# The last group's division in a mixer-attention kernel: sums moved by DMA, division on VectorE, eight jobs kept in halves of score buffers

## The chip, the core and the metric

The kernel runs on one core of one Trainium2 chip. The metric is device time in microseconds (us) of one execution; lower is better. Five engines of the core work side by side, each through its own queue in order: TensorE (PE, matmuls into PSUM), VectorE (DVE), ScalarE (ACT), GpSimd (POOL) and SyncE (SP, which here only issues DMAs). PSUM is used here as eight banks of 128 x 512 float32.

## The reference

Two kinds of blocks alternate, twice each with the same weights, on `x` of 2048 tokens by 512 channels; each block gets a layer norm of `x`, and its result is added to `x`.

```python
def _A_ref(x, wq, wk, wv, wo):              # 32 heads of 16, one shared key and value head
    q = (x @ wq).reshape(B, S, H, Dh).transpose(0, 2, 1, 3)
    k, v = x @ wk, x @ wv
    p = softmax(einsum("bhqd,bkd->bhqk", q, k) * Dh ** -0.5)
    o = einsum("bhqk,bkd->bhqd", p, v)
    return o.transpose(0, 2, 1, 3).reshape(B, S, H * Dh) @ wo
def _B_ref(x, w1, b1, w2, b2):              # token mixing: the MLP runs over the 2048 tokens
    h = layernorm(x)
    u = gelu(einsum("bsd,sf->bdf", h, w1) + b1)      # F = 1792
    return (einsum("bdf,fs->bds", u, w2) + b2).transpose(0, 2, 1)

x = A_x
x = x + _A_ref(layernorm(x), ...); x = x + _B_ref(layernorm(x), ...)
x = x + _A_ref(layernorm(x), ...); x = x + _B_ref(layernorm(x), ...)
```

## The kernel before

All tokens stay in SBUF as 16 row tiles `x0` to `x15` of 128 x 512. A float32 product is made of three matmuls: each operand is split into a rounded first part (a cast) and the rest (a subtract), and the product of the two rests is left out.

**Attention.** 32 groups (4 blocks of 512 queries by 8 groups of 4 heads) each make scores into double banks (`bank2`, tag `sc`, three buffers of two banks each, so six banks), exponentials on ACT, and sums into one of the two remaining banks (`bank`, tags `ac0` and `ac1`). The sums hold for each head the weighted values and the sums of weights in alternating rows. When a group's sums are done, `finish` copies them to SBUF (`ev`, line 696), and two DMAs move even and odd rows apart into a tile `o` for two groups: `o[:, 0]` has values, `o[:, 1]` the sums of weights (line 704). `division` then makes, for four slices of 128 columns, a reciprocal, a product, a cast and a subtract on DVE, and leaves them as `hl`. `project` multiplies `hl` by `wo` for one row tile and adds it to `x` on DVE (lines 762 and 765).

**The mixer's first product** begins during attention. Its unit is a half job: six matmuls that take one tile of `w1` (256 tokens by 128 columns, `w1r`, 128 KB by DMA) and two normed row tiles `hb`; two half jobs with the same 128 columns of `u` make a job, which is added by DVE into `uacc` (`ua`, line 1023). `following` is called after each half job: it splits the weight tile three half jobs ahead (in the tail a cast on ACT and a subtract on POOL, lines 1000 and 1002) and issues the load of the one seven ahead. There are 84 half jobs (42 jobs) for the first three blocks of tokens (`self.inner`); the 28 half jobs of the last block need its normed rows and come afterwards.

**The tail.** The methods run in the order in which they are written, and every engine takes its part of that order. `Mixer.rest`, called once per layer, does what is left after the last scores: the two remaining row tiles of the last projection but one (in a bank of `ac`), the last sums, the nine jobs that are left (66 to 82), the division of the last two groups, the last projection, the norm of the last four row tiles, and then the loop over the last block (`pu_l`, 168 matmuls), followed by the second product (`py`).

The last two groups go another way than the others there. `finish` keeps their `ev`, and `last_rows` moves even and odd rows apart by matmuls with columns of the identity into two score buffers (line 733), once for each group, the second time after four jobs. `last_division` copies the values on ACT, inverts on DVE from PSUM, multiplies and subtracts on POOL and casts on ACT (lines 744 to 750). The jobs run between these steps, each added to `ua` as soon as it is done, but for the last three. The last norm takes for each row tile a norm on DVE, a cast on ACT and a subtract on DVE or POOL in turn (lines 1121 to 1125).

Of the kernel before, what the change touches and what calls it, by code (L numbers as in the profile page):

```python
# [8 lines left out]
F32 = mybir.dt.float32  # L9
# [9 lines left out]
P = 128  # L19
S, D, H, DH, F = 2048, 512, 32, 16, 1792  # L20
NB = 4
# [31 lines left out]
def kernel(  # L53
# [612 lines left out]
    class Attention:  # L666
        def __init__(self, layer):
            self.l = layer
            self.pp = pool(f"weights{layer}", side="right")
            self.ohl, self.acc, self.pend = {}, {}, []  # L670
            self.drained, self.finished, self.late = 0, [], []
# [19 lines left out]
        def finish(self, i):  # L691
# [5 lines left out]
            if i >= NB * NG - 2:  # L697
                self.late.append(ev)
                return
# [26 lines left out]
        def last_rows(self):  # L726

            if not hasattr(self, "rows"):
                self.rows = [bank2(f"rows{self.l}_{k}")[:, 0, :] for k in range(2)]
                self.moved = 0  # L730
            r = 64 * self.moved
            for k in (1, 0):
                nc.tensor.matmul(  # L733
                    self.rows[k][r : r + 64, :], ident[:, k:P:2], self.late[self.moved],
                    start=True, stop=True, skip_group_check=True,
                )
            self.moved += 1

        def last_division(self):

            p, n, m = self.pool, self.l, NB * ND - 1
            o, d = (p.tile([P, 2, QB], F32, tag="o", bufs=2, name=f"o{n}_l{k}")[:, 0, :] for k in range(2))
            hl = self.ohl[m] = p.tile([P, 2, QB], F32R, tag="hl", bufs=2, name=f"hl{n}_{m}")
            nc.scalar.copy(o, self.rows[0])
            for t in range(4):
                c = slice(t * P, (t + 1) * P)
                nc.vector.reciprocal(d[:, c], self.rows[1][:, c])
                nc.gpsimd.tensor_tensor(o[:, c], o[:, c], d[:, c], op=ALU.mult)  # L748
                nc.scalar.copy(hl[:, 0, c], o[:, c])
                nc.gpsimd.tensor_tensor(hl[:, 1, c], o[:, c], f32(hl[:, 0, c]), op=ALU.subtract)  # L750
# [148 lines left out]
    class Mixer:  # L899
# [160 lines left out]
        def projection(self, att, which):  # L1060
# [3 lines left out]
            att.project(parts, t, bank(which, f"po{n}_{parts[0]}_{t}"))  # L1064
# [15 lines left out]
        def rest(self, att):  # L1080
# [4 lines left out]
            def job(pu=None):  # L1085

                j = self.done // 2
                if pu is None:
                    pu = bank(j, f"pu{n}_{self.done}")
                self.product(pu, stop=False)  # L1090
                self.following()
                r, f = self.product(pu, start=False)
                self.following()
                return pu, r - 1, f

            while self.projections:
# [321 lines left out]
```

## Time and profile before

| | |
|---|---|
| median of three runs | 2607.62 us (2606.88 to 2608.09) |
| the profiled execution's own time | 2608.36 us |
| its span, first to last instruction | 2606.2 us |
| mean granted TensorE clock | 0.994 |
| PE busy | 2567.8 us, 99% |
| ACT busy | 2122.6 us, 81% |
| DVE busy | 818.2 us, 31% |
| POOL busy | 142.5 us, 5% |

A row of a timeline has the start and the duration in us, the engine, the line of the kernel, the operation, what it writes and reads, and how many were merged; in brackets stands how long the engine was idle before it and what ended that. `PEld` is the loading of weights, which lies beside matmuls. A table by windows has for each window its length, then busy time and number of instructions of PE, PEld, DVE, ACT and POOL, the granted clock (1.00 is full), the busy share of the DMA engines and GB/s. In the rows of one line, three numbers with slashes are the shortest, median and longest duration in ns.

### The profile page before, as it was taken

What the parts mean: (1) busy time and instruction counts of PE and PEld (TensorE: products, weight loads), DVE (VectorE), ACT (ScalarE), POOL (GpSimd) and SP (SyncE); (2) the same over time, 40 slices, a digit from 0 to 9 for tenths busy, and PEclk for the clock granted to TensorE, in tenths of its full rate; (3) what the DMA queues carried; (4) which work ended last, traced back from release to release, by engine and by line L of the source; (5) the groups of instructions that cost most, each with busy time, mean ns of one, the idle gap of its engine ahead of it and who ended that gap; (6) DMA issues with size and microseconds to landing.
All of it is one profiled execution on the core that took longest, in us unless ns stands there. A gap on an engine that the chain in (4) does not pass through costs nothing. (4 is left out here: it accounts for less than half of the span.)

```text
span 2606.2 us, 41310 instructions
## 1 busy us (share of the span) xinstructions
PE 2567.8 (99%) x16168; PEld 1244.7 (48%) x16168; DVE 818.2 (31%) x1847; ACT 2122.6 (81%) x2368; POOL 142.5 (5%) x209
## 2 busy tenths in 40 slices
PE   7999999999999999999999999999999999999999
PEld 6344333444344444478873333434443444445887
DVE  6122242223222432254441222322242223323432
ACT  5889999999999999763239999999999999995511
POOL 2000000000000000141000000000000000002300
PEclk8999999999999999999999999999999999999999
DMA  3221201111111111034423110111111111101343
GB/s 98 67 64 48 62 27 42 30 42 32 38 30 38 31 40 30 19 99 117 130 60 106 53 47 28 31 38 30 38 30 38 30 38 33 42 25 37 114 124 96
DMA packets 167631, 138.24 MB, mean 53 GB/s; under 512 B 17378, under 2 KB 132096, under 8 KB 167168
## 3 DMA queue, kind: packets, MB, share of 16 engines
q1 hardware_dynamic: 167424, 135.48, 18.0%
q8 instruction: 131, 2.15, 0.4%
q14 instruction: 76, 0.62, 0.1%
HBM read 95.57 MB, written 24.12 MB: 46 GB/s over the span
## 5 line engine op out<-in xcount | busy, mean ns | idle before, releaser
L780 ACT ACTIVATE p<-sc 128x1024 f32<-128x1024 f32 x2048 | 1918.0, 1030 | 115.9 <-PE sc L773 115.9
L786 PE MATMUL acc<-p,vaug 128*32 128x512 f32 x8192 | 1012.6, 599 | 0.0
L773 PE MATMUL sc<-qs,kst 51*128 51x512 f32 x4096 | 724.2, 439 | 11.8 <-ACT p L780 3.4
L773 PEld LDWEIGHTS sc<-qs,kst 51*128 51x128 f32 x4096 | 325.8, 184 | 650.4 <-ACT p L780 378.0
L786 PEld LDWEIGHTS acc<-p,vaug 128*32 128x32 f32 x8192 | 227.3, 109 | 447.6 <-issue 407.3
L1195 PE MATMUL py<-u,w 128*128 128x512 f32 x1344 | 307.6, 390 | 0.0
L1195 PEld LDWEIGHTS py<-u,w 128*128 128x128 f32 x1344 | 251.9, 188 | 52.3
L1015 PE MATMUL pu<-hb,w 128*128 128x512 f32 x984 | 265.9, 409 | 0.4 <-POOL w L1002 0.4
L1015 PEld LDWEIGHTS pu<-hb,w 128*128 128x128 f32 x984 | 173.8, 188 | 85.0 <-issue 50.8
L1183 ACT CAST w<-w2r 128x896 fp32r<-128x896 f32 x64 | 60.3, 945 | 182.0 <-PE py L1195 170.3
L1023 DVE TENSOR_TENSOR ua<-ua,pu 128x512 f32<-128x512 f32 x54 | 37.0, 688 | 405.1 <-PE pu L1015 405.1
L1002 POOL TENSOR_TENSOR w<-w1r,w 128x256 fp32r<-128x256 f32 x86 | 68.4, 809 | 1699.6 <-ACT w L1000 1698.4
L765 DVE TENSOR_TENSOR x<-x,po 128x512 f32<-128x512 f32 x64 | 44.0, 688 | 306.9 <-PE po L762 306.9
L716 DVE RECIPROCAL o<-o 128x128 f32<-128x128 f32 x120 | 113.5, 946 | 12.3 <-DMA o<-ev 12.3
L696 DVE COPY ev<-acc 128x512 f32<-128x512 f32 x64 | 44.1, 689 | 214.1 <-PE acc L786 214.1
L1021 DVE COPY ua<-pu 128x512 f32<-128x512 f32 x28 | 19.4, 692 | 286.3 <-PE pu L1015 286.3
L1184 DVE TENSOR_TENSOR w<-w2r,w 128x896 fp32r<-128x896 f32 x64 | 71.5, 1119 | 104.7 <-ACT w L1183 104.6
L762 PE MATMUL po<-wo,hl 128*128 128x512 f32 x360 | 100.7, 413 | 1.6 <-DVE x L765 1.6
L353 PE MATMUL pq<-hT,wq 128*128 128x512 f32 x336 | 89.9, 417 | 0.0
L1015 PE MATMUL pu_l<-hb,w 128*128 128x512 f32 x336 | 82.0, 404 | 2.9 <-POOL hb L1125 1.7
L431 DVE CAST q<-pq 128x512 fp32r<-128x512 f32 x24 | 16.6, 692 | 208.8 <-PE pq L353 163.7
L762 PEld LDWEIGHTS po<-wo,hl 128*128 128x128 f32 x360 | 62.7, 188 | 36.3 <-issue 20.3
(166 smaller groups left out, 1048.7 us busy)
## 6 DMA issues: line engine op xcount, KB each, us to landing
w1r<-in_B_w_dram SPq DMA_DIRECT2D x224, 128.0 KB
w2r<-in_B_w_dram SPq DMA_DIRECT2D x64, 448.0 KB
qs<-qd SPq DMA_DIRECT2D x384, 64.0 KB
qd<-q SPq DMA_DIRECT2D x64, 256.0 KB
o<-ev SPq DMA_DIRECT2D x120, 128.0 KB
x<-in_A_x_dram SPq DMA_DIRECT2D x16, 256.0 KB
out_dram<-x SPq DMA_DIRECT2D x16, 256.0 KB
wqr<-in_A_wq_dram SPq DMA_DIRECT2D x4, 512.0 KB
```

What stands on the lines that cost most here:

```text
L353: yield nc.tensor.matmul(out, a, c, start=(k == 0), stop=(k == len(terms) - 1))
L696: nc.vector.tensor_copy(ev, acc)
L716: nc.vector.reciprocal(o[:, 1, c], o[:, 1, c])
L762: nc.tensor.matmul(po, a, c, start=(k == 0), stop=(k == 3 * len(parts) - 1))
L773: nc.tensor.matmul(sc[:, j, :], kst[kt // 4][rows, kt % 4 * P : (kt % 4 + 1) * P], qs[i % NQ][rows, j0 // 2, :], start=True, stop=True,)
L780: nc.scalar.activation(pt, sc, AF.Exp, scale=0.25)
L786: nc.tensor.matmul(self.acc[i][c : c + 32, :], vaug[:, kt].rearrange("p d k -> p (d k)"), pt[:, j, :], start=(kt == 0), stop=(kt == NKT - ...
L1002: eng.tensor_tensor(w[:, 1], raw, f32(w[:, 0]), op=ALU.subtract)
L1015: nc.tensor.matmul(pu, a, c, start=(start and k == 0), stop=(stop and k == 5))
L1183: nc.scalar.copy(w[:, 0], raw)
L1184: nc.vector.tensor_tensor(w[:, 1], raw, f32(w[:, 0]), op=ALU.subtract)
L1195: nc.tensor.matmul(py, a, d, start=(c == 0 and f == 0 and k == 0), stop=(c == 1 and f == NFH - 1 and k == 2),)
```

## The change

- `finish` treats the last two groups as all others: their sums go by two DMAs each into the shared tile `o`. `last_rows` is gone.
- `last_division` works on `o` in SBUF: reciprocal, product and subtract on DVE, the cast on ACT. It is a generator: one slice of columns is issued before a job and one after each of its half jobs, so its steps stand between those of two jobs.
- In `rest` the second of the remaining row tiles of the projection takes a score bank and not the bank of the first one.
- One job is added at once. The other eight are kept (`late`): two in `ac` banks (`pu_a`, `pu_b`) and six in halves of three score buffers (`pu_m`, `pu_l` twice). Two of the eight stand before the last projection and six behind it.
- The last projection runs as four row tiles in a row, two to a score buffer.
- The last norm goes by pairs of row tiles. Casts and subtracts are on DVE, but for one cast on ACT; after each pair four of the kept jobs are added.

```diff
@@ finish
-            if i >= NB * NG - 2:
-                self.late.append(ev)
-                return
             if i % 2 == 0:
                 self.o = p.tile([P, 2, QB], F32, tag="o", bufs=2, name=f"o{n}_{i}")
@@ last_rows is left out; last_division
-            o, d = (p.tile([P, 2, QB], F32, tag="o", bufs=2, name=f"o{n}_l{k}")[:, 0, :] for k in range(2))
+            o = self.o
             hl = self.ohl[m] = p.tile([P, 2, QB], F32R, tag="hl", bufs=2, name=f"hl{n}_{m}")
-            nc.scalar.copy(o, self.rows[0])
-            for t in range(4):
-                c = slice(t * P, (t + 1) * P)
-                nc.vector.reciprocal(d[:, c], self.rows[1][:, c])
-                nc.gpsimd.tensor_tensor(o[:, c], o[:, c], d[:, c], op=ALU.mult)
-                nc.scalar.copy(hl[:, 0, c], o[:, c])
-                nc.gpsimd.tensor_tensor(hl[:, 1, c], o[:, c], f32(hl[:, 0, c]), op=ALU.subtract)
+            cols = [slice(t * P, (t + 1) * P) for t in range(4)]
+
+            def second(c):
+                nc.vector.tensor_tensor(hl[:, 1, c], o[:, 0, c], f32(hl[:, 0, c]), op=ALU.subtract)
+
+            for t, c in enumerate(cols):
+                nc.vector.reciprocal(o[:, 1, c], o[:, 1, c])
+                nc.vector.tensor_tensor(o[:, 0, c], o[:, 0, c], o[:, 1, c], op=ALU.mult)
+                nc.scalar.copy(hl[:, 0, c], o[:, 0, c])
+                if t:
+                    second(cols[t - 1])
+                yield
+            second(cols[3])
+            yield
@@ projection
-            att.project(parts, t, bank(which, f"po{n}_{parts[0]}_{t}"))
+            name = f"po{n}_{parts[0]}_{t}"
+            att.project(parts, t, bank2(name)[:, 0, :] if which is None else bank(which, name))
@@ rest
+            which = att.spare()
             while self.projections:
-                self.projection(att, att.spare())
-            att.drain(2)
-            att.last_rows()
+                self.projection(att, which)
+                which = None
             att.drain(len(att.pend))
-            while self.done < self.inner - 2 * KEPT:
-                self.add(*job())
-            self.add(*job())
-            att.last_rows()
-            att.last_division()
-            self.add(*job())
+            free = NB * NG % 2
+            jobs = (self.inner - self.done) // 2
+            for k in range(jobs - 8):
+                self.add(*job(bank(free + k, f"pu{n}_e{k}")))
+            free += jobs - 8
+            division = att.last_division()
+            next(division)
+            late = [job(bank(free, f"pu{n}_a"), division)]
+            mid = half(f"pu{n}_m")
+            late.append(job(mid[0], division))
...
             for t in range(4):
-                att.project([NB * ND - 1], t, bank2(f"po{n}_l{t}")[:, 0, :])
+                if t % 2 == 0:
+                    po = half(f"po{n}_l{t}")
+                att.project([NB * ND - 1], t, po[t % 2])
                 nc.vector.bn_stats(st[:, t, :], x[4 * b + t])
                 nc.vector.bn_aggr(mv[:, t, :], st[:, t, :])
-                if t == 1:
-                    self.add(*job())
-            late = [job(), job(), job(bank2(f"pu{n}_j")[:, 0, :])]
+            late.append(job(mid[1]))
+            late.append(job(bank(free + 1, f"pu{n}_b")))
+            for k in range(2):
+                late += [job(pu) for pu in half(f"pu{n}_l{k}")]
             y = rstd(mv, True, f"b{n}_l")
-            for t in range(4):
...
+            for ts_, first in ((0, 1), (1, 2, 4, 5)), ((2, 3), (0, 3, 6, 7)):
+                tmps = []
+                for t in ts_:
+                    tmp = self.wp.tile([P, D], F32, tag="ht", bufs=2, name=f"ht{n}_{4 * b + t}")
+                    normed(tmp, 4 * b + t, mv, y, t)
+                    tmps.append(tmp)
+                for t, tmp in zip(ts_, tmps):
+                    r = 4 * b + t
+                    h = self.h[r] = self.hp.tile([P, 2, D], F32R, tag="h", bufs=6, name=f"hb{n}_{r}")
+                    (nc.scalar.copy if t == 3 else nc.vector.tensor_copy)(h[:, 0, :], tmp)
+                    nc.vector.tensor_tensor(h[:, 1, :], tmp, f32(h[:, 0, :]), op=ALU.subtract)
+                for k in first:
+                    self.add(*late[k])
```

`half(name)` takes one score buffer and gives its two banks; `job(pu, between)` runs two half jobs into `pu` and, where `between` is given, takes one step of it after each.

39 lines of the change are left out of this document (11 added, 28 removed).

## The prediction

> **What bounds the kernel now.** I read the page first, then TensorE's (PE) timeline through the stretch that the change rewrites, then those of VectorE (DVE) and GpSimd (POOL), then a table of TensorE's clock by windows.
>
> ```profile
> span 2606.2 us, 41310 instructions
> ...
> PE 2567.8 (99%) x16168; PEld 1244.7 (48%) x16168; DVE 818.2 (31%) x1847; ACT 2122.6 (81%) x2368; POOL 142.5 (5%) x209
> ```
>
> PE is busy for 99% of the span, so a change counts by the PE work and the PE waits that it takes out or puts in. This one lies in `rest`, which runs once per layer. PE's timeline there, layer 0 (start, duration, operation, idle before it and what ended that):
>
> ```profile
> 1084.59 0.97 PE L762 MATMUL po<-wo,hl 128*128 128x512 f32 x3
> 1086.34 0.96 PE L762 MATMUL po<-wo,hl 128*128 128x512 f32 x3 [0.78 <-DVE x L765]
> 1087.23 1.07 PE L786 MATMUL acc<-p,vaug 128*32 128x512 f32 x8
> 1088.23 1.94 PE L733 MATMUL rows<-ev,ident 128*64 128x512 f32 x4
> 1090.09 11.20 PE L1015 MATMUL pu<-hb,w 128*128 128x512 f32 x48
> 1101.22 1.93 PE L733 MATMUL rows<-ev,ident 128*64 128x512 f32 x4
> 1103.08 3.02 PE L1015 MATMUL pu<-hb,w 128*128 128x512 f32 x12
> ...
> 1112.23 5.64 PE L1015 MATMUL pu<-hb,w 128*128 128x512 f32 x24
> 1117.71 2.88 PE L1015 MATMUL pu_j<-hb,w 128*128 128x512 f32 x12
> 1120.49 0.49 PE L1015 MATMUL pu_l<-hb,w 128*128 128x512 f32 x1
> ...
> 1123.67 39.26 PE L1015 MATMUL pu_l<-hb,w 128*128 128x512 f32 x164 [0.85 <-POOL hb L1125]
> 1162.77 2.46 PE L1195 MATMUL py<-u,w 128*128 128x512 f32 x10
> ```
>
> The same first and last rows in layer 1:
>
> ```profile
> 2371.72 0.97 PE L762 MATMUL po<-wo,hl 128*128 128x512 f32 x3
> ```
> ```profile
> 2449.88 5.42 PE L1195 MATMUL py<-u,w 128*128 128x512 f32 x23
> ```
>
> The stretch takes 78.18 us in layer 0 (1084.59 to 1162.77) and 78.16 in layer 1, so one sum serves both. Dense, 24 matmuls take 5.48 us (1112.23 to 1117.71), 0.228 each: a job (12) takes 2.74, a row tile of the last projection (3) 0.68, the last block (168) 38.3.
>
> **What goes, per layer.** (a) The second `po` waits until 1086.34 for the first one's bank. In the score bank that it gets now it follows at 1084.59 + 0.68 = 1085.27: 1.07. What is late next is DVE, free just in time (rows below). (b) The last sums are no longer moved by identity matmuls, 1088.23 to 1090.09 and 1101.22 to 1103.08: 1.86 each, 3.72. (c) From 1103.08 to 1112.23 go 9.15 us for 36 matmuls (two jobs, four row tiles; 8.21 dense). The 0.94 stand where weight splits queue behind the old division on ACT and POOL; I count 0.85 and leave the rest to changes between forms. (d) From 1120.49 to the first `py` go 42.28 us for 38.3 of work: 3.98, because the last normed rows `hb` come late. Together 9.6. (d) goes only if the rows are ready in the changed order; checked below.
>
> **What comes instead.** The last sums take the road of all other groups: the copy `ev`, two DMAs, the division. First the DVE rows that say when `ev` can start, then a place where the division waited for nothing but the DMA:
>
> ```profile
> 1085.60 0.69 DVE L765 TENSOR_TENSOR x<-x,po 128x512 f32<-128x512 f32 x1 [18.40 <-PE po L762]
> 1087.34 0.69 DVE L765 TENSOR_TENSOR x<-x,po 128x512 f32<-128x512 f32 x1 [1.05 <-PE po L762]
> 1088.36 0.69 DVE L696 COPY ev<-acc 128x512 f32<-128x512 f32 x1 [0.34 <-PE acc L786]
> ```
> ```profile
> 1559.11 0.69 DVE L696 COPY ev<-acc 128x512 f32<-128x512 f32 x1 [7.20 <-PE acc L786]
> 1563.37 0.95 DVE L716 RECIPROCAL o<-o 128x128 f32<-128x128 f32 x1 [3.57 <-DMA o<-ev]
> 1564.36 0.29 DVE L719 TENSOR_TENSOR o<-o 128x128 f32<-128x128 f32 x1
> 1564.69 0.23 DVE L720 CAST hl<-o 128x128 fp32r<-128x128 f32 x1
> 1564.95 0.29 DVE L721 TENSOR_TENSOR hl<-o,hl 128x128 fp32r<-128x128 f32 x1
> 1565.16 0.94 DVE L716 RECIPROCAL o<-o 128x128 f32<-128x128 f32 x1
> ```
>
> `acc` starts 0.89 after the second `po` (1086.34 to 1087.23), at 1086.16; `ev` 1.13 later (1087.23 to 1088.36), at 1087.29, to 1087.98. The first add ends at 1086.29 and the second stands from then to 1086.98, so neither holds `ev` up. From the end of `ev` to the first reciprocal are 3.57: 1091.55. PE starts jobs 1.00 after `acc` (1087.23 to 1088.23), at 1087.16, and runs three, `pu_e`, `pu_a` and the first half of `pu_m`, until 1095.38. On SP's queue the two DMAs stand ahead of the load of weight tile 73, which now waits for `ev` too. That tile's split stands on ACT behind the third column's cast, near 1096, over 6 us after the load can go: no cost.
>
> DVE's order in the built program is reciprocal, product, next reciprocal, next product, subtract for the column before, and so on over four columns. With 0.99 from reciprocal to product (1563.37 to 1564.36) and 0.21 to 0.25 from each short operation to the next (0.21 from 1564.95 to 1565.16), it takes 4 x 0.99 + 8 x 0.24 = 5.9, and about 0.1 more because the last subtract waits for ACT's cast of its column. ACT's other casts lie beside reciprocals. So the first add of `x` starts at 1097.55.
>
> Now a new wait. Row tiles 0 and 1 of the last projection share one score buffer, tiles 2 and 3 another, and in the built program the first matmul of a second half waits for the add that reads the first half. PE's queue is in order: behind that matmul stand the other row tiles and six jobs, and behind those everything. Adds with statistics between them:
>
> ```profile
> 1106.84 0.69 DVE L765 TENSOR_TENSOR x<-x,po_l 128x512 f32<-128x512 f32 x1
> ...
> 1108.39 0.65 DVE L765 TENSOR_TENSOR x<-x,po_l 128x512 f32<-128x512 f32 x1
> ```
>
> Tile 0 ends on PE at 1095.38 + 0.68 = 1096.06. Tile 1 follows the add, 1097.55 + 0.69 + 0.05 (0.05 as from 1086.29 to 1086.34) = 1098.29: 2.23 idle. Tile 2 follows at once, to 1099.65. The add for tile 1 starts 1.00 after its matmuls do (1086.34 to 1087.34), at 1099.29, that for tile 2 then 1.55 later (1106.84 to 1108.39), at 1100.84, and tile 3 goes at 1101.58: 1.93 idle. Together 4.16. Six jobs follow from 1102.3, 16.4 long, to 1118.7.
>
> Are the normed rows there by then? Before, the first stood 8.26 us after the last `po_l` (1112.23 to 1120.49); now that is 1110.6, and rows 12 and 13 need three more DVE operations of about an add's 0.69, so 1113 at the latest: a cover of over 5 us for the cast moved from ACT to DVE and the subtract moved from POOL. Rows 14 and 15 wait for the last job to free their buffers, but PE wants them only 12 matmuls (2.74) after the jobs, and their four operations fit there. The eight adds of the kept jobs fill DVE behind these and free banks wanted 5.5 after the jobs. If one of these covers fails, each us is PE idle.
>
> **DVE against POOL.** Products and subtracts move from POOL to DVE while POOL goes on splitting weights. Four rows from four answers: a split; a long POOL operation, until 1197.17; the usual time of one DVE subtract; the same subtract beside that POOL operation:
>
> ```profile
> 1093.65 0.74 POOL L1002 TENSOR_TENSOR w<-w1r,w 128x256 fp32r<-128x256 f32 x1 [0.65 <-ACT w L1000]
> 1191.56 5.61 POOL L279 TENSOR_TENSOR wq<-wqr,wq 128x1024 fp32r<-128x1024 f32 x2 [0.28 <-ACT wq L278]
> L1184 DVE TENSOR_TENSOR w<-w2r,w x64: 1083/1092/2623, 1154.4 to 2589.1; 128x896 fp32r<-128x896 f32 x64
> 1195.50 2.62 DVE L1184 TENSOR_TENSOR w<-w2r,w 128x896 fp32r<-128x896 f32 x1
> ```
>
> A subtract of 1.09 took 2.62 there: it waited for POOL. After each of the first three columns' casts ACT releases a weight split (0.74 on POOL) that begins shortly before the next product is due. So three blocks of 0 to 0.74 stand on the chain, 0 to 2.2 in all; by their places some 0.4, 0.2 and 0.2, and I take 0.75. The Trainium skill (SBUF — State Buffer, Who interferes with whom) says that a VectorE operation with two SBUF inputs and a GpSimd operation that reads SBUF shut each other out for a whole instruction; the 2.62 agrees. Without that rule the sum would be 1.5 us lower over both layers.
>
> **The clock.** Windows of one clock step each (length, PE busy; PEclk is the third figure from the end):
>
> ```profile
> 21.98:25.40 3.42, 2.28 (x21) 2.04 (x20) 2.25 (x7) 2.94 (x5) 1.52 (x8) 1.00 0.00 0
> 25.40:28.81 3.41, 2.92 (x16) 2.54 (x17) 3.41 (x6) 0.93 (x2) 2.67 (x12) 1.00 0.00 0
> ```
> ```profile
> 1121.08:1124.49 3.41, 2.05 (x7) 1.17 (x8) 2.83 (x6) 1.17 (x2) 1.27 (x1) 1.00 0.16 43
> 1124.49:1127.90 3.41, 3.41 (x10) 2.63 (x9) 1.15 (x2) 2.16 (x5) 1.27 (x1) 0.50 0.00 0
> ```
>
> After 3.41 us with PE busy for 2.05 the next 3.41 ran at half clock, 1.7 us of (d); after 2.28 the clock stayed. The new gaps, 1096.1 to 1102.3 with 1.4 us of matmuls between, put such a step almost wherever the steps fall. So a drop comes back, for 0.8 to 2.6 us by how the steps lie; I take 1.7.
>
> **Sum.** 9.6 - 4.16 - 0.75 - 1.7 = 3.0 per layer, 6.0 in all. The profiled execution took 2608.36 (span 2606.2 and 2.2 around it); it would take 2602.4, and against the median of 2607.62 the forecast is 2601.6. A measurement of this kernel can tell about 0.2%, 5.2 us, from no change: this is faster by little more than that.
>
> **Rivals.** (1) The clock stays up, since no single gap is a whole step long: the longest is 2.23 + 0.75 = 2.98. The gain is 4.7 per layer: 2598.2, and 2597 with lighter blocks by POOL. The step that was busy for 2.05 speaks against it. The Trainium skill (TensorE: Matmul & The Clock Gate, What's actually happening) lets the clock fall after an idle window of about 3.4 us; read strictly that is this rival, and the row at 1121.08 speaks against the strict reading. Chance 0.25. (2) The chain from `ev` to tile 3 is longer, by landing, blocks or a second slow step: all of that is PE idle. With 2 us more per layer: 2605.6. Chance 0.20. (3) Slower: the DMA lands late. Each us of that is a us of PE in each layer; from 3.0 later nothing is gained, from 5.6 later it is slower by over 0.2%. At three times 3.57 it is 2601.6 + 2 x 7.14 = 2615.9. Against it: nothing else is on the queue there. Chance 0.05. (4) The change doesn't do what it orders the rows for: `hb` is late again, (d) stays, and 9.6 - 3.98 is eaten up by the 4.9 of new gaps and a clock drop: 2609.6. Against it: 5 us of cover. Chance 0.04. The forecast, 2599.5 to 2604, has 0.46.
>
> **Range and chances.** 2597 to 2605.6 leaves out about one in ten on each side. Faster by over 0.2% (below 2602.4): rival 1 and some 0.33 of the forecast's 0.46, so 0.58; within 0.2%: the rest of it, rival 2 and half of rival 4, 0.35; slower 0.07.
>
> **What would show it.** Right: no `rows` matmuls; the first reciprocal of `o` 3.3 to 3.9 after `ev` ends; PE idle 2.2 to 3.2 and about 1.9 before the second and fourth row tile of `po_l`, ended by DVE `x`; a clock of 0.50 behind them and none at the first `pu_l`; 38.3 from there to `py`. Wrong: a reciprocal over 5 us after `ev`, a `pu_l` that waits for `hb`, or gaps under 1 us at `po_l`.

## The result and the profile after

| | before | after |
|---|---|---|
| median | 2607.82 us (2606.88 to 2608.52, 8 runs) | 2600.25 us (2598.03 to 2601.11, 8 runs) |
| the profiled execution: time, span | 2608.36, 2606.2 us | 2601.11, 2599.4 us |
| from the first `po` to the first `py`, layer 0, layer 1 | 78.18, 78.16 us | 74.99, 75.67 us |

The changed kernel is faster by 0.3%: ratio 0.9969 with a 95% interval of 0.9959 to 0.998. The page of the changed kernel:

```profile
span 2599.4 us, 41307 instructions
...
PE 2555.0 (98%) x16152; PEld 1241.3 (48%) x16152; DVE 830.7 (32%) x1873; ACT 2117.2 (81%) x2360; POOL 132.6 (5%) x189
```

TensorE's timeline, layer 0, from the second-last projection to the second product:

```profile
1084.51 1.65 PE L753 MATMUL po<-wo,hl 128*128 128x512 f32 x6
1086.09 1.07 PE L777 MATMUL acc<-p,vaug 128*32 128x512 f32 x8
...
1095.38 0.87 PE L753 MATMUL po_l<-wo,hl 128*128 128x512 f32 x3
1098.96 2.62 PE L753 MATMUL po_l<-wo,hl 128*128 128x512 f32 x6 [2.71 <-DVE x L756]
1102.69 1.62 PE L753 MATMUL po_l<-wo,hl 128*128 128x512 f32 x3 [1.11 <-DVE x L756]
1104.11 3.86 PE L1006 MATMUL pu_m<-hb,w 128*128 128x512 f32 x12
...
1110.54 49.12 PE L1006 MATMUL pu_l<-hb,w 128*128 128x512 f32 x216
1159.50 2.70 PE L1202 MATMUL py<-u,w 128*128 128x512 f32 x11
```

The second `po` follows the first at once (one row, x6), there are no `rows` matmuls, and `pu_l` runs to `py` in one row of 216 without a wait for `hb`. In their place stand two idle times that ended with an add to `x`, ahead of row tiles 1 and 3. The rows around them are slow: three matmuls in 1.62 where 0.87 is usual, twelve in 3.86 where 2.88 is. The table by windows, cut at the clock's steps, says why (third from the end is the granted clock):

```profile
1095.80:1099.22 3.42, 0.71 (x3) 0.30 (x3) 3.19 (x8) 1.51 (x5) 1.70 (x4) 1.00 0.30 87
1099.22:1102.63 3.41, 2.36 (x6) 1.30 (x5) 2.69 (x7) 0.00 (x0) 0.48 (x1) 0.51 0.27 78
1102.63:1106.04 3.41, 3.35 (x8) 2.71 (x9) 2.42 (x6) 0.00 (x0) 0.00 (x0) 0.50 0.00 0
```

A window with PE busy for 0.71 is followed by two at half clock, 6.83 us. Layer 1 has the same two, 2382.6 to 2389.5. The chain that sets the first idle time, on DVE:

```profile
1087.22 0.69 DVE L696 COPY ev<-acc 128x512 f32<-128x512 f32 x1 [0.34 <-PE acc L777]
...
1091.49 0.95 DVE L734 RECIPROCAL o<-o 128x128 f32<-128x128 f32 x1 [0.65 <-DMA o<-ev]
1092.47 0.29 DVE L735 TENSOR_TENSOR o<-o 128x128 f32<-128x128 f32 x1
...
1093.66 0.71 DVE L735 TENSOR_TENSOR o<-o 128x128 f32<-128x128 f32 x1
...
1095.47 0.51 DVE L735 TENSOR_TENSOR o<-o 128x128 f32<-128x128 f32 x1
...
1097.08 0.49 DVE L735 TENSOR_TENSOR o<-o 128x128 f32<-128x128 f32 x1
...
1098.14 0.68 DVE L756 TENSOR_TENSOR x<-x,po_l 128x512 f32<-128x512 f32 x1
```

From the end of `ev` to the first reciprocal are 3.58, from there to the add of row tile 0 6.65. The four products took 0.29, 0.71, 0.51 and 0.49.

The profiled executions differ by 7.25 us. The two stretches give 3.19 and 2.49 of that, 0.45 stands outside the spans, and 1.1 lies elsewhere inside them, between the two stretches (from the first `py` of layer 0 to the first `po` of layer 1). One place there shows in the windows: around the start of layer 1, from 1355 to 1370 us, before ran at a mean clock of 0.77, and after at 1.00. The change does not touch that place. How the clock's steps fall there differs between the traces (none, one or two windows at half clock); I count that part as no effect of the change.

### The profile page after: what moved, and what is told of

It reads as the page before. It is cut to its first block, busy times and chain, and to the rows that moved or that the text cites. A ratio compares the mean times of both kernels' runs of the same rounds, so it can differ in the third digit from the quotient of the medians.

```text
span 2599.4 us, 41307 instructions
## 1 busy us (share of the span) xinstructions
PE 2555.0 (98%) x16152; PEld 1241.3 (48%) x16152; DVE 830.7 (32%) x1873; ACT 2117.2 (81%) x2360; POOL 132.6 (5%) x189
## 5 line engine op out<-in xcount | busy, mean ns | idle before, releaser
L1006 PE MATMUL pu<-hb,w 128*128 128x512 f32 x792 | 219.4, 412 | 0.0
L1006 PEld LDWEIGHTS pu<-hb,w 128*128 128x128 f32 x792 | 138.4, 188 | 72.4 <-issue 47.5
L1014 DVE TENSOR_TENSOR ua<-ua,pu 128x512 f32<-128x512 f32 x38 | 26.2, 689 | 382.0 <-PE pu L1006 382.0
L1006 PE MATMUL pu_l<-hb,w 128*128 128x512 f32 x432 | 98.2, 389 | 0.0
L1006 PEld LDWEIGHTS pu_l<-hb,w 128*128 128x128 f32 x432 | 81.1, 188 | 16.8
```

What stands on the lines that cost most here:

```text
L1006: nc.tensor.matmul(pu, a, c, start=(start and k == 0), stop=(stop and k == 5))
```

## The experiments

Each was timed in at least five runs beside before. In the last column are the stretches from first `po` to first `py` of the profiled run, layer 0 and 1, and in brackets the windows at half clock in each stretch.

| run | median us (range) | ratio to before, 95% interval | stretches (slow windows) |
|---|---|---|---|
| the changed kernel | 2600.25 (2598.03 to 2601.11) | 0.9969, 0.9959 to 0.998 | 74.99, 75.67 (2, 2) |
| e1 dummies | 2596.52 (2595.36 to 2596.62) | 0.9956, 0.9943 to 0.997 | 73.07, 73.06 (0, 0) |
| e2 crossed | 2596.42 (2595.07 to 2598.55) | 0.9957, 0.9943 to 0.997 | 72.80, 74.49 (1, 2) |
| e3 four buffers | 2591.25 (2590.47 to 2592.42) | 0.9938, 0.9925 to 0.9952 | 69.73, 70.11 (0, 0) |
| e4 job first | 2595.55 (2595.21 to 2596.26) | 0.9954, 0.994 to 0.9968 | 72.16, 73.61 (1, 0) |
| e5 dense | 2591.21 (2590.06 to 2592.42) | 0.9938, 0.9924 to 0.9951 | 70.44, 70.86 (0, 0) |
| e6 identity | 2597.84 (2596.36 to 2599.01) | 0.9964, 0.995 to 0.9977 | 73.93, 73.88 (0, 0) |
| e7 sums first | 2597.70 (2597.1 to 2599.24) | 0.9963, 0.9949 to 0.9976 | 72.27, 75.45 (0, 2) |
| e8 splits later | 2599.24 (2594.72 to 2601.34) | 0.9964, 0.995 to 0.9977 | 72.60, 76.05 (0, 2) |
| e9 second po | 2604.72 (2603.93 to 2606.74) | 0.9991, 0.9982 to 1.0001 | 77.19, 77.13 (0, 1) |
| e10 one more kept | 2609.20 (2608.25 to 2610.32) | 1.0005, 0.9996 to 1.0014 | 78.58, 78.56 (0, 1) |
| e11 dense, second form | 2589.24 (2587.23 to 2589.31) | 0.993, 0.9916 to 0.9944 | 68.70, 69.23 (0, 0) |
| e12 engines back | 2609.61 (2606.49 to 2611.76) | 1.0007, 0.9998 to 1.0016 | 75.96, 76.25 (0, 0) |

**What the waits at the row tiles cost.** e1, on the changed kernel:

```diff
                 if t % 2 == 0:
                     po = half(f"po{n}_l{t}")
+                for _ in range((0, 9, 0, 5)[t]):
+                    h = self.h[11]
+                    nc.tensor.matmul(mid[1], h[:, 0, :P], h[:, 0, :], start=True, stop=True)
                 att.project([NB * ND - 1], t, po[t % 2])
```

> The changed kernel with matmuls that compute nothing needed (9 ahead of row tile 1, 5 ahead of row tile 3, into the half of a score buffer whose job comes later), so that TensorE is busy while it waits for the adds. Nothing on the chain from the sums to the row tiles is changed. Theory (the waits also cost a clock drop of 6.83 us in each layer of the profiled run, by which the add after row tile 1 comes 0.4 to 0.5 later, row tile 3 takes 1.42 instead of 0.68 and the half job behind it 3.7 instead of 2.73): no window at 0.50 there, 2.1 less per layer, 4.2 less in all against a run with that drop, somewhat less against runs where it is shorter; idle before row tiles 1 and 3 together below 1.5. Rival (the drop is cheap, because TensorE waits there anyway): the clock stays up but the time is within 1 us of the changed kernel's.

```profile
1095.45 0.86 PE L753 MATMUL po_l<-wo,hl 128*128 128x512 f32 x3
1096.15 2.25 PE L1117 MATMUL pu_m<-hb 128*128 128x512 f32 x9
1099.09 1.63 PE L753 MATMUL po_l<-wo,hl 128*128 128x512 f32 x6 [0.69 <-DVE x L756]
...
1102.41 0.93 PE L753 MATMUL po_l<-wo,hl 128*128 128x512 f32 x3 [0.53 <-DVE x L756]
1103.18 2.92 PE L1006 MATMUL pu_m<-hb,w 128*128 128x512 f32 x12
```

Row tile 1 still starts where it did, 3.64 after row tile 0 (3.58 in the changed kernel), so the dummies hide none of the wait itself. But no window is at half clock: row tile 3 starts 0.35 sooner after row tile 0, the next job follows it after 0.77 instead of 1.42, and that job takes 2.92 instead of 3.86. The stretches are 1.92 and 2.61 shorter, the median 3.7. Not all of the 2.61 is the clock: in layer 1 of the changed kernel the first reciprocal came 4.25 after `ev`, in e1 3.64, and that lies ahead of row tile 1. From the start of row tile 1 to the first `py` the changed kernel takes 60.54 in both layers, and e1 58.55 and 58.52. So the clock drop alone costs the profiled run 2.0 per layer. Two windows at half clock would cost a TensorE that is always busy 3.4, half of the 6.83; part of them lies in waits.

e2 and e3 change the buffers of the row tiles:

```diff
-                if t % 2 == 0:
-                    po = half(f"po{n}_l{t}")
-                att.project([NB * ND - 1], t, po[t % 2])
+            po = [half(f"po{n}_l{t}") for t in range(2)]                       # e2, ahead of the loop
+                att.project([NB * ND - 1], t, po[t % 2][t // 2])
+            po = [half(f"po{n}_l0")[0], bank(free + 1, f"po{n}_l1"),           # e3, ahead of the loop
+                  half(f"po{n}_l2")[0], mid[1]]
+                att.project([NB * ND - 1], t, po[t])
```

In e3 the jobs behind them come in the order l0, l0, l1, l1, b, m, and their adds accordingly.

> The changed kernel with the four row tiles of the last projection crossed over the two score buffers: tile 0 in the first, 1 in the second, 2 in the second half of the first, 3 in that of the second. Theory (tiles 1 and 3 wait because they share a buffer with the tile before them): tile 1 follows tile 0 within 0.3, tile 2 waits some 2.0 for the add of tile 0, tile 3 some 0.9 for that of tile 1; idle 2.9 instead of 4.0 and the end of tile 3 some 3.0 earlier at full clock; with a clock drop at tile 2 between 0.2 and 1.9 earlier. In all 2 to 5 us less than the changed kernel. Rival (what is waited for is the division, whatever the buffers): the last row tile ends where it did, time within 1 us.

> The changed kernel with a buffer of its own for each of the four row tiles: the first halves of two score buffers, the bank of a job that now comes behind, and the half whose job now comes last; the kept jobs come in the order l0, l0, l1, l1, b, m. Theory (the waits at the row tiles are for shared buffers; only the division remains): the row tiles end about 1099.2 in layer 0 instead of 1104.1, TensorE is busy for some 2.6 of the window before it and the clock stays up; normed rows are ready 3 us before they are wanted. 4.9 less per layer, about 9.8 in all: 2590. Rival (the division is the longer chain): tiles wait for its columns instead, less than 2 us per layer gained.

```profile
1096.41 1.56 PE L753 MATMUL po_l<-wo,hl 128*128 128x512 f32 x6
1099.99 0.93 PE L753 MATMUL po_l<-wo,hl 128*128 128x512 f32 x3 [2.02 <-DVE x L756]
1101.51 1.37 PE L753 MATMUL po_l<-wo,hl 128*128 128x512 f32 x3 [0.59 <-DVE x L756]
```
```profile
1096.18 2.02 PE L753 MATMUL po_l<-wo,hl 128*128 128x512 f32 x8
1098.63 0.50 PE L753 MATMUL po_l<-wo,hl 128*128 128x512 f32 x1 [0.43 <-DVE hl L731]
1098.96 0.86 PE L753 MATMUL pu_m<-wo,hl 128*128 128x512 f32 x3
1099.68 11.18 PE L1006 MATMUL pu_l<-hb,w 128*128 128x512 f32 x48
```

Crossed (first fence), tile 1 follows tile 0, and tiles 2 and 3 wait 2.02 and 0.59, both for adds. With four buffers (second fence) the only wait left that the profile names is 0.43, and it is for the division's last column (`hl`). The row tiles are through 3.50 after they begin instead of 8.73. So the waits were the shared buffers', as the prediction read from the built program; the division alone costs 0.8 (3.50 for 2.74 of matmuls). e2 came out 3.8 below the changed kernel, e3 9.0, where 2 to 5 and 9.8 were expected.

**Hiding the division under a job.** e4 puts the job `mid[1]` ahead of the row tiles:

```diff
+            late.append(job(mid[1]))
+            x0, x1 = half(f"po{n}_l0"), half(f"po{n}_l2")
+            po = [x0[0], bank(free + 1, f"po{n}_l1"), x1[0], x0[1]]
             for t in range(4):
...
-            late.append(job(mid[1]))
-            late.append(job(bank(free + 1, f"pu{n}_b")))
             for k in range(2):
                 late += [job(pu) for pu in half(f"pu{n}_l{k}")]
+            late.append(job(bank(free + 1, f"pu{n}_b")))
```

> The changed kernel with the second job of the middle buffer put ahead of the row tiles (2.74 of TensorE work while the division ends) and row tiles 0 to 3 in four places of which only the last two share a buffer (three tiles apart). Theory (TensorE idle and the clock drop at the row tiles were 6.9 per layer: 15.2 from the first row tile to the last block's start with 8.2 of matmuls and a half job's rest): TensorE dense through the row tiles, 6.9 less per layer, 2586.5, if the normed rows still come in time; the cover for them shrinks from 5 us to about 1. Rival (the cover is gone: rows or banks come late at the last block): a wait of 1 to 3 us per layer at the first or second pu_l, 2589 to 2593.

```profile
1102.88 12.73 PE L1006 MATMUL pu_l<-hb,w 128*128 128x512 f32 x48 [1.84 <-DVE x L756]
...
1118.17 38.24 PE L1006 MATMUL pu_l<-hb,w 128*128 128x512 f32 x168
```

The row tiles are dense (12 matmuls from 1098.12 on in 2.93), but a wait that neither side had named took the place of theirs: the first job behind them wants a score buffer that row tile 2 holds until its add is done, 1.84. The rows and banks of the last block came in time: 168 matmuls in 38.24 with no wait in layer 0 (in layer 1 weights were late, by 0.51 at `pu_m` and 0.39 in the last block). The median, 2595.55, is above both ranges. e5 therefore puts `pu_b` first, whose bank is free sooner, and adds `pu_a` early, so that its bank serves row tile 3:

```diff
+            self.add(*late[0])
             x0, x1 = half(f"po{n}_l0"), half(f"po{n}_l2")
-            po = [x0[0], bank(free + 1, f"po{n}_l1"), x1[0], x0[1]]
+            po = [bank(free + 1, f"po{n}_l1"), x0[0], x1[0], bank(free, f"po{n}_l3")]
```

> The kernel of the job-first run mended at the place where it waited: the job pu_a is added to ua while VectorE waits for the first row tile, so that its bank takes row tile 3; row tile 0 takes the bank of pu_b, tiles 1 and 2 first halves of two score buffers; pu_b follows the row tiles, ahead of the four pu_l jobs. Theory (in the job-first run 1.84 us per layer went to a job whose buffer still held a row tile, and 1.6 to the clock drop behind it in one layer): no wait at or behind the row tiles, from the second po to py 68.6 per layer against 75.0 and 75.7 in the changed kernel, 2587. Rival (the cover of the normed rows and banks, about 1 us in the sum, is gone): waits of 1 to 2 at the first pu_l matmuls of the last block, 2589 to 2591.

```profile
1115.13 39.43 PE L1006 MATMUL pu_l<-hb,w 128*128 128x512 f32 x168 [0.59 <-DVE ua L1014]
```

No wait at or behind the row tiles, but 0.59 for a bank at the last block, and the block's 168 matmuls take 39.43 instead of 38.24: the rival came nearest (2591.21 against its 2589 to 2591), the cover was used up, and the median is e3's. e11 mends that: `pu_m` is added before the row tiles' adds, and the norm of rows 12 and 13 is issued ahead of the last two kept jobs (code against that of e5, abridged).

```diff
             self.add(*late[0])
+            self.add(*late[1])
...
-            for k in range(2):
-                late += [job(pu) for pu in half(f"pu{n}_l{k}")]
+            late += [job(pu) for pu in half(f"pu{n}_l0")]
             y = rstd(mv, True, f"b{n}_l")
+            norm((0, 1))                       # casts on ScalarE, subtracts on VectorE
+            late += [job(pu) for pu in half(f"pu{n}_l1")]
+            for k in (2, 4, 5): self.add(*late[k])
+            norm((2, 3))                       # the cast of row 14 on VectorE
+            for k in (3, 6, 7): self.add(*late[k])
```

> The kernel of the dense run with the last waits taken out: the first pu_m is added with pu_a ahead of the row tiles' adds, the norm of rows 12 and 13 (casts on ScalarE) is issued ahead of the last two kept jobs, and after it only pu_m and the two of the first pu_l buffer are added before the norm of rows 14 and 15. Theory (0.59 for a bank and about 1 inside the last block, for rows 14 and 15, were left per layer): no waits from the second po to py, 68.7 per layer instead of 70.4 and 70.9, 2587.5. Rival (casts on ScalarE hold up the weight splits queued behind them, or the second norm stays late): a wait of 0.5 to 1.5 moves to the weights or rows, 2589 to 2591.

Layer 0's stretch came out at 68.70, the forecast; layer 1's at 69.23. The median, 2589.24, is 1.7 above the forecast and inside the rival's range, although the waits that the rival named are not in layer 0. It is the fastest version here.

**What the DMA road is worth.** e6 moves the sums of both groups by identity matmuls again, right after the last sums. The division's first step then also goes one job earlier, ahead of `pu_e`; `last_rows` is left out here:

```diff
+            rows = half(f"rows{n}")
+            att.last_rows(rows)                # for both kept ev: rows[k][r:r+64] <- ident[:, k::2], ev
+            division = att.last_division(rows) # values copied to o on ScalarE
+            next(division)
...
-                nc.vector.reciprocal(o[:, 1, c], o[:, 1, c])
+                nc.vector.reciprocal(o[:, 1, c], rows[1][:, c])
```

> The changed kernel with the sums of the last two groups moved by identity matmuls again (both right after the last sums, ahead of the jobs; values copied on ScalarE, reciprocals from PSUM), the division on VectorE and the kept jobs as they are. Theory (the DMA road takes 3.72 of matmuls off TensorE and gives part of it back as waits at the row tiles): row tiles start 3.7 to 4.0 later, the division is done before them, the wait at tile 1 is 1.0 instead of 2.9; at full clock 2.1 later per layer, with the drop shorter than in the changed kernel 0.9: 2602 to 2604.5. Rival A (the removed matmuls are worth their whole 3.72): 2607.7. Rival B (the DMA road saves nothing, its waits eat it up): 2600 or less.

```profile
1085.99 2.82 PE L730 MATMUL rows<-ev,ident 128*64 128x512 f32 x8
1088.74 3.02 PE L1019 MATMUL pu_e<-hb,w 128*128 128x512 f32 x12
...
1098.77 1.60 PE L766 MATMUL po_l<-wo,hl 128*128 128x512 f32 x6 [0.87 <-DVE x L769]
```

Rival B came true (2597.84 against 2600 or less): by the medians the DMA road is 2.4 slower than the identity matmuls; the intervals overlap, so what is safe is that it is not faster by the 7.4 of the removed matmuls. Eight of them in a row take 2.75 (1085.99 to 1088.74), not 3.72, and the idle time ahead of row tile 1 falls from 2.71 to 0.87. Compared where no window is slow, the DMA road is 0.8 per layer ahead (73.07 and 73.06 in e1, 73.93 and 73.88 in e6). The clock takes that back: the mean granted clock was 0.993 to 0.996 in the runs of the changed kernel, 0.995 to 0.997 in those of e6.

**Two parts of the chain.** e7 issues the DMA of the sums of weights first, e8 puts three weight splits behind the division:

```diff
-            for k in range(2):
+            for k in (1, 0) if i == NB * NG - 1 else range(2):      # e7
```
```diff
-                self.following()                                     # e8, after the second half of pu_a
+                held.append(self.done - 1)                           # and both halves of pu_m
...
+            for j in held:                                           # e8, after the division's last step
+                self.split1(j + 3)
+                self.load1(j + 7)
```

> The changed kernel with the two DMAs of the last group in the other order: the sums of weights, which the reciprocals read, first, the values second. Theory (the first reciprocal waits for the DMA that is issued second, one issue of 0.55 behind the first): the reciprocal starts some 0.5 sooner after ev, 3.0 instead of 3.58, and each row tile's wait falls by that: 0.5 less per layer, about 1 in all. Rival (both land together, by what they share): no change in the distance from ev to the reciprocal.

> The changed kernel with three of the four weight splits that stand between the columns of the division (a cast on ScalarE and a subtract on GpSimd each) put behind it. Theory (GpSimd and VectorE shut each other out: the products took 0.71, 0.51 and 0.49 where 0.29 is usual): the third and fourth product take 0.29, the division ends some 0.4 sooner, 0.4 less per layer, 0.8 in all, apart from the clock. Rival (the products are slow for another reason, such as the reciprocal ahead of them): durations stay at 0.5.

```profile
1090.88 0.69 DVE L1014 TENSOR_TENSOR ua<-ua,pu_e 128x512 f32<-128x512 f32 x1 [2.22 <-PE pu_e L1006]
1091.50 0.95 DVE L734 RECIPROCAL o<-o 128x128 f32<-128x128 f32 x1
```
```profile
1093.37 0.70 DVE L735 TENSOR_TENSOR o<-o 128x128 f32<-128x128 f32 x1
...
1095.17 0.29 DVE L735 TENSOR_TENSOR o<-o 128x128 f32<-128x128 f32 x1
...
1096.57 0.29 DVE L735 TENSOR_TENSOR o<-o 128x128 f32<-128x128 f32 x1
```

e7 (first fence): the reciprocal no longer waits for the DMA but follows the add of `pu_e`, 2.85 after `ev`; the idle time ahead of row tile 1 is 1.99 instead of 2.71. The theory holds for the mechanism. The 2.5 by the medians is more than the 1 expected, and in the profiled run layer 0 kept its clock. e8 (second fence; the same three products took 0.71, 0.51 and 0.49 in the changed kernel): the two products whose splits are gone take 0.29, the one whose split stayed 0.70. That shows the price of POOL beside the division, 0.2 for each of the two, and the idle time ahead of row tile 1 falls to 2.27 in layer 0. In time e8 is 1.0 below the changed kernel, within the spread of the runs.

**Where (a) and (d) come from.** e9 is before with the second `po` in a score buffer, e10 before with one job moved:

```diff
-            att.project(parts, t, bank(which, f"po{n}_{parts[0]}_{t}"))                              # e9
+            att.project(parts, t, bank2(name)[:, 0, :] if which is None else bank(which, name))
```
```diff
-                if t == 1:                                                                           # e10
-                    self.add(*job())
-            late = [job(), job(), job(bank2(f"pu{n}_j")[:, 0, :])]
+            both = bank2(f"pu{n}_j")
+            late = [job(), job(), job(both[:, 0, :]), job(both[:, 1, :])]
```

> The kernel before with one edit: the second of the two remaining row tiles takes a score buffer, as in the changed kernel, and not the bank of the first. Theory (the second po waited for the add that reads the first, 1.07 per layer, and nothing else is late behind it): acc starts 1.6 instead of 2.64 after the first po, the rest shifts by that, 1.07 less per layer, 2605.4 against 2607.5. Rival (the last normed rows come no sooner, since other work sets them): the wait at pu_l grows by what the po wait lost, no change.

> The kernel before with one edit: the job between row tiles 1 and 2 of the last projection goes behind row tile 3 and is kept with the other three, added after the second normed row. Nothing of the sums' road or the division is changed. Theory (the 3.98 at the last block are a matter of how many jobs stand behind the row tiles): adds of tiles 2 and 3 come some 2.8 sooner, the wait at pu_l and its clock drop all but go, tiles 2 and 3 wait some 1.1 for the old division's columns: 1.5 to 3 less per layer, 2602 to 2604.5. Rival (the normed rows are late by ScalarE and GpSimd, which are queued with weight splits, and not by the row tiles): the wait at pu_l stays above 2 and with the new waits the time is that of before or more.

e9 did what the theory says: 0.99 and 1.03 less in the stretches, 2.9 by the medians, though its interval just reaches no change. It shows one thing more, about (d). In its layer 0 no window is at half clock, and a new wait for POOL's subtract of a row stands inside the last block:

```profile
1125.23 35.21 PE L1015 MATMUL pu_l<-hb,w 128*128 128x512 f32 x152 [0.84 <-POOL hb L1128]
1160.28 4.94 PE L1198 MATMUL py<-u,w 128*128 128x512 f32 x21
```

From its first `pu_l` at 1117.92 to `py` it takes 42.36 us all the same; its layer 1, with a window at half clock, takes 42.28, as before did. e10 repeats this: 42.82 without such a window, 42.81 with one. Where TensorE waits for late rows, the half clock cost nothing.

In e10 my theory fell and the rival held: the last block still waits some 4.5 (42.82 for 38.3 of work), and the time is 1.6 above before. Its ACT rows:

```profile
1120.27 0.41 ACT L1000 CAST w<-w1r 128x256 fp32r<-128x256 f32 x1 [0.95 <-PE pu_j L1015]
1120.58 0.62 ACT L1122 CAST hb<-ht 128x512 fp32r<-128x512 f32 x1
```

The normed row `ht` was there at 1119.38, but its cast on ACT stands behind the split of a weight tile, and that waits for the job `pu_j` on TensorE to free its buffer (1120.27, ended by PE). A job more ahead of the block moves this cast back by itself. In before the cast followed its row at once: the norm on DVE ran from 1119.23 for 0.55, and the cast began 0.04 later.

```profile
1119.82 0.62 ACT L1123 CAST hb<-ht 128x512 fp32r<-128x512 f32 x1
```

So ACT's queue did not yet hold this row up there; it is a limit that lies right beside, and takes over as soon as the row comes sooner. So another explanation of what the change gains at (d) was left: not the jobs, but the engines. e12 is the changed kernel with the engines of before for the last rows:

```diff
-                    (nc.scalar.copy if t == 3 else nc.vector.tensor_copy)(h[:, 0, :], tmp)
-                    nc.vector.tensor_tensor(h[:, 1, :], tmp, f32(h[:, 0, :]), op=ALU.subtract)
+                    nc.scalar.copy(h[:, 0, :], tmp)
+                    eng = nc.gpsimd if t % 2 else nc.vector
+                    eng.tensor_tensor(h[:, 1, :], tmp, f32(h[:, 0, :]), op=ALU.subtract)
```

> The changed kernel with the casts and subtracts of the last four normed rows on the engines of before (all casts on ScalarE, the subtracts of rows 13 and 15 on GpSimd); six jobs still stand behind the row tiles and are kept. Theory (after the one-more-kept run: what made the rows late before was their place in ScalarE's and GpSimd's queues behind the weight splits, which TensorE's progress paces, so more jobs in front don't help): the cast of row 12 starts at about 1120.6, behind the split for the last kept job, the waits at pu_l come back, some 2.3 per layer and in most runs a clock drop of 1.7: 2605 to 2608.5. Rival (the six jobs behind the row tiles are the cover, whichever engine does it): no wait at pu_l, time within 1.5 us of the changed kernel's 2600.

```profile
1109.89 1.42 DVE L201 TENSOR_SCALAR ht<-x,mvb_l,rw_b_l 128x512 f32<-128x512 f32 x2
1120.05 0.81 DVE L1134 TENSOR_TENSOR hb<-ht,hb 128x512 fp32r<-128x512 f32 x1 [8.74 <-ACT hb L1132]
```
```profile
1119.09 0.41 ACT L991 CAST w<-w1r 128x256 fp32r<-128x256 f32 x1 [0.95 <-PE pu_l L1006]
1119.40 1.14 ACT L1132 CAST hb<-ht 128x512 fp32r<-128x512 f32 x2
```
```profile
1122.20 3.93 PE L1006 MATMUL pu_l<-hb,w 128*128 128x512 f32 x16 [1.83 <-DVE ua L1014]
```

Two rows were normed by 1111.3. Their casts stood on ACT behind the splits of weight tiles, the last of which waited for a matmul of `pu_l`, and began at 1119.40. DVE waited 8.74 for them, and behind the subtract in DVE's queue stood the adds that free the banks; TensorE waited 1.83 for one of these. By the medians all of the change's gain is gone (2609.61, 1.1 above the upper end that I expected), with the same six kept jobs behind the row tiles as in the changed kernel. The profiled run, the fastest of its eleven (2606.49), shows only part of that loss. Its stretches have no window at half clock; against e1's, which have none either, they are 2.9 and 3.2 longer (in layer 1 some 0.2 of it is a later landing). Seven of the other runs had a lower mean clock (0.992 to 0.994 against 0.995), and where their clock dropped no trace shows. These 2.9 and 3.2 are what bears out the theory: the kept jobs give time, but only to operations that do not stand in a queue behind work paced by those same jobs. It is the place in the queue that counts and not the engine's name; e11 agrees with that. There ACT casts rows 12 and 13, but their casts are issued ahead of the last two kept jobs, so that ACT waits for the norm only and TensorE not at all (216 matmuls of `pu_l` in 49.31):

```profile
1109.58 1.14 ACT L1134 CAST hb<-ht 128x512 fp32r<-128x512 f32 x2 [1.64 <-DVE ht L201]
```

## Why the prediction was right, and where it was not

The time came out 1.35 below the forecast of 2601.6, inside the likeliest case. Per layer:

| step | forecast | measured (layer 0, layer 1 where both are known) |
|---|---|---|
| (a) second `po` | 1.07 | 0.99, 1.03 (e9) |
| `acc` to `ev`; `ev` to reciprocal | 1.13; 3.57 | 1.13; 3.58, 4.25 |
| reciprocal to the add of row tile 0 | 6.75 with POOL's blocks (6.00 and 0.75) | 6.65, 6.64 |
| POOL's blocks | 0.4, 0.2, 0.2 | 0.42, 0.22, 0.20 |
| all at full clock: what goes less the waits and blocks | 9.6 - 4.16 - 0.75 = 4.7 | 5.11, 5.10 (e1: 78.18 to 73.07, 78.16 to 73.06) |
| the clock drop | 1.7 (0.8 to 2.6) | 1.99, 2.02 (row tile 1 to `py`, against e1) |
| later landing than in e1 | nothing | 0, 0.6 |
| net | 3.0 | 3.19, 2.49 |

- **Two terms were mis-sized, and that they nearly cancel is luck.** The clock drop cost 2.0 per layer and not 1.7. The prediction took one slow window, as in before. The profiled run has two in each layer: the wait for the second shared buffer falls into the first slow window and keeps it from being full, and in the stretches a first slow window that was not full was always followed by a second (last section). At full clock 0.4 more was gained than the 4.7 of the sum. The prediction's own times had this: its jobs end at 1118.7, 38.3 for the last block and 0.75 for POOL's blocks lead to 1157.75, and that is 73.2 after the first `po`, where e1 measured 73.07. The list of what goes came out 0.3 lower, since it is a separate count that took only 0.85 of the 0.94 in (c) and left out small changes between forms.
- **In layer 1 the sums came 0.67 later,** and with them the weight splits, which stand on ACT behind the division's casts and which the prediction put at no cost:

```profile
2376.38 0.30 ACT L736 CAST hl<-o 128x128 fp32r<-128x128 f32 x1 [4.29 <-DVE o L735]
2376.59 0.40 ACT L991 CAST w<-w1r 128x256 fp32r<-128x256 f32 x1
```

  The first `pu_m` job took 3.50 there instead of 2.88. In the changed kernel this adds nothing, since row tile 1 waits for the division in any case; in e11, whose row tiles do not wait, the two `pu_m` jobs of layer 1 took 6.77 instead of 6.02 and its stretch is 0.53 longer.
- **Step (d) had the right size, and its reason was short in two places.** The prediction called 1.7 of the 3.98 a matter of the clock; e9 and e10 have the same block without the slow window and no faster, so it was all wait for the late rows. And it counted the move of casts and subtracts to DVE as a cost of nothing under five microseconds of cover from six jobs. e10 and e12 show that the move is the larger part of the gain in this form: with the old engines the same six jobs lose 2.9 and 3.2. Whether the new engines do with three jobs behind the row tiles, as before had, wasn't tried. The cover was real all the same: e4 ran with one job less behind the row tiles and the rows of the last block came in time.
- **Step (b), 3.72 for the identity matmuls, was right as a count** and told little of their worth. Together they cost 2.75 when issued in a row, and what replaced them costs nearly as much at full clock (e6), more with the drop. Step (c) had no run of its own.
- **Rival 1, the clock stays up,** is what e1 forces: 2596.5, where the rival said 2598.2. Without dummies the idle of 2.9 before row tile 1, shorter than a window, brought the clock down in both layers of the profiled run; the page of the Trainium skill (TensorE: Matmul & The Clock Gate, What's actually happening) read strictly, a drop after an idle window, does not hold here. In e7 and e8 layer 0 kept the clock (1.99 and 2.27 idle there), and layer 1 did not (2.78 and 2.38). Nor is it the length of the gap alone: in e12 the same gap, 2.70 and 2.78, kept the clock in both layers. There it lies across two windows (PE busy for 2.21 and 1.62 in layer 0), where the changed kernel had one with 0.71. So the drop is in part a matter of where the windows fall, as the range of 0.8 to 2.6 allowed.
- **Rival 2** happened in small: the second slow window that it named came in both layers, and in layer 1 the 0.67. Rivals 3 and 4 did not. The lock that the prediction drew from the Trainium skill (SBUF — State Buffer, Who interferes with whom) agrees with e8: without a split beside it a product takes 0.29.

## What to carry to other kernels

A wait is worth more than its length when it drops the clock: here 3.8 us of idle time per layer cost 2.0 more. It is not so where TensorE waits for something else in any case: the slow window in the last block of before cost nothing (e9, e10). Here ordinary work put into the idle time (a job moved ahead, e11) or buffers of their own (e3) gave more than the whole change. Jobs kept in reserve hide late rows only if the operations that make the rows do not stand in a queue behind work that waits for those same jobs; look for what stands ahead of them in each queue. And before a transfer replaces matmuls, ask who waits for its end: 3.7 us of matmuls per layer were taken off TensorE, and against the same matmuls issued in a row 0.8 was gained at full clock.

## What the runs showed of the hardware

- **Half clock can last two windows.** After the drop in layer 0 of the changed kernel the next window had PE busy for 2.36 of 3.41 and the clock stayed at 0.50 for another; where a whole slow window was busy (e4, below, 3.41) it was over after one. In the stretches of these traces five first slow windows with PE busy for 1.8 to 2.8 were followed by a second, and six that were busy for 3.3 or more were not; why is not shown.
- **Where the bound for a drop lies, the busy time does not tell.** In the stretches, windows with PE busy for 0.65 to 1.32 were all followed by 0.50. Between 1.58 and 2.05 both occur: first e4 with 1.58 and a drop, then e6 with 1.70 and none; before had a drop after 2.05. Around the start of layer 1, e1 had one even after 2.26 (1353.03 to 1356.44). What else decides stays open.

```profile
1100.16:1103.58 3.42, 1.58 (x7) 1.02 (x7) 3.25 (x8) 0.00 (x0) 0.59 (x1) 1.00 0.45 131
1103.58:1106.99 3.41, 3.41 (x10) 2.64 (x9) 3.10 (x12) 0.40 (x1) 0.73 (x1) 0.50 0.00 0
```
```profile
1099.55:1102.96 3.41, 1.70 (x8) 1.14 (x7) 3.03 (x7) 0.00 (x0) 0.00 (x0) 1.00 0.26 75
1102.96:1106.37 3.41, 3.41 (x17) 2.79 (x16) 3.04 (x10) 0.81 (x2) 0.76 (x2) 1.00 0.00 0
```

- **The two DMAs landed later in layer 1.** In the nine traces that issue them as the changed kernel does, the first reciprocal came 3.57 to 3.62 after `ev` in layer 0, and 3.64 (e1) to 4.80 (e4, e8) in layer 1. With the sums first it was 3.94 in layer 1 against at most 2.85. Why is not settled.
